# A decode step of attention and feed-forward: 72 rows of thirty value tiles weighed row by row on ScalarE and summed on GpSimd, and 56 rows left to TensorE

## The chip, the cores and the metric

The kernel runs on one core of one Trainium2 chip. A core has five engines that run their own queues of instructions in order: TensorE (PE), VectorE (DVE), ScalarE (ACT), GpSimd (POOL) and SyncE (SP), which here issues the DMAs. The metric is the device time of one execution in microseconds (us); lower is better. The kernel before takes 1319.18 us, the median of three runs (1319.18 to 1319.35).

## The reference

Four sequences (B = 4) decode one token each. A modulation vector scales and shifts a layer norm; 32 heads of 128 attend over 4096 cached positions; a feed-forward layer with SiLU follows. All is float32, and nearly all bytes are the two caches, 268 MB each.

```python
mod = (_silu(c) @ w_mod).reshape(c.shape[0], 6, 1, -1)
sa, ca, ga, sb, cb, gb = (mod[:, i] for i in range(6))
h = _layernorm(x, axis=-1) * (1 + ca) + sa
q = (h @ wq).reshape(B, Sq, H, Dh).transpose(0, 2, 1, 3)
scores = jnp.einsum("bhqd,bhkd->bhqk", q, k_cache) * (Dh ** -0.5)
p = _softmax(scores, axis=-1)
o = jnp.einsum("bhqk,bhkd->bhqd", p, v_cache)
x = x + ga * (o.transpose(0, 2, 1, 3).reshape(B, Sq, H * Dh) @ wo)
h = _layernorm(x, axis=-1) * (1 + cb) + sb
x = x + gb * (_silu(h @ w1) @ w2)
```

## The kernel before

**Tiles.** The loop `for n in range(N)` runs over 32 tiles. Tile n holds four heads (group t = n // 4) of one sequence (b = n % 4): Kn and Vn are each one load of 8.39 MB, 128 partitions by 128 rows of 128 numbers. A head has 32 partitions, and a partition has 128 neighbouring positions (NJ = 128 rows). Below, "K16" or "V14" is the tile of that n.

**Scores.** `mult` multiplies K by the query in place, rows 0 to 39 on GpSimd (NA = 40; the query is in SBUF, `qw`), the other 88 on VectorE (the query is in PSUM, `qb`); line L280 is both. `red` (L285) sums each row on VectorE: first its own 88 rows, then GpSimd's 40. `rowmax`, `bmax` (a transpose on PE, L293) and `negmax` (L298 to L301) find the largest score of each head; `softexp` takes Exp on ScalarE (L307), with the sums of a tile in column b of `rs`, and writes the weights on GpSimd (L311) into the padded masks `pz`, 16 columns for each set of four rows (JJ = 4).

**Values.** For tiles 0 to 29 (`first(n)` is not 0), `vmult` weighs the first NV = 32 rows on GpSimd with one product of 4096 numbers a partition (L323), and folds them to four rows by three sums of 2048, 1024 and 512 (L327). `vsum` adds those four rows into the accumulator `po` by a matmul with a mask of heads (L333), and `pv` multiplies the other 96 rows by `pz`, four rows a matmul, 24 matmuls (L348; each matmul appears twice in the trace). Tiles 30 and 31 leave all 128 rows to `pv`.

**Order.** The program writes the order of each engine by hand; no scheduler moves anything. One iteration n issues, in this order: the load of K(n+1); the K products of n; the query of n+1 (`make_qb`, on ScalarE L275, and at the last tile of a group L269); `vmult` and `pv` of n-1; the reductions of n; the load of Vn; `rowmax` and `bmax` of n; `vsum` of n-1; `negmax` and `softexp` of n. Three buffers of 64 KB a partition (`bufs=3`) hold all tiles: Vn takes the buffer of Kn when that is reduced, and K(n+1) takes the buffer of V(n-2) when `vsum(n-2)` is done. The loads land in the order K(n), V(n-1), K(n+1), V(n), and all are issued from SyncE's queue (L85).

**Group work.** At b = 3 the iteration also runs `gather(t, 0)` and `norm(t)`. `norm` adds the softmax sums of the group by a matmul on PE, and then VectorE takes the reciprocal. For groups 0 to 3 (t < TA = 4) that is the matmul L383, the reciprocal L386 and a product of two small SBUF tensors, L387 (32x32). For groups 4 to 7 it is the matmul L392, a product with a PSUM operand (L394), a reduction (L396) and a reciprocal (L397). On PE these matmuls stand behind `vsum(n-1)`; on VectorE they stand ahead of the next tile's K product. At b = 1 comes `gather(t-1, 1)`, at b = 2 `spread(t-1)`.

Of the kernel before, what the change touches and what calls it, by code (L numbers as in the profile page):

```python
# [10 lines left out]
AF = mybir.ActivationFunctionType  # L11
# [6 lines left out]
def kernel(  # L18
# [10 lines left out]
    nc = tc.nc  # L29
    P = 128  # L30
    B, H, S, Dh = kc.shape
# [12 lines left out]
    JJ = 4  # L44
    NG = NJ // JJ
    HG = NG // 2
# [4 lines left out]
    FG = F // G  # L51
    NA = 40
    NL = 56
    NV = 32
    SCALE = 1.0 / math.sqrt(Dh)
    EPS = 1e-5
    N = B * NT
# [29 lines left out]
    kt, vt = {}, {}  # L87
# [189 lines left out]
    sc, nm, po, rs = {}, {}, {}, {}  # L277
# [25 lines left out]
    def softexp(n):  # L303
        t, b = divmod(n, B)
        if b == 0:
            rs[t] = work.tile([P, B], F32, tag="rs", name=f"rs{t}")
        nc.scalar.activation(sc[n], sc[n], AF.Exp, bias=nm[n], accum_out=rs[t][:, b : b + 1])  # L307
        for h in range(2):
            f = first(n) if h == 0 else 0
            m = HG - f  # L310
            nc.gpsimd.tensor_mul(  # L311
                pz[h][:, f * W : HG * W].rearrange("p (g x) -> p g x", g=m)[:, :, E:].rearrange("p g (i j) -> p g i j", i=HP),
                sc[n][:, JJ * (HG * h + f) : HG * JJ * (h + 1)].rearrange("p (g j) -> p g j", j=JJ)
                .unsqueeze(2).to_broadcast([P, m, HP, JJ]),
                hm.unsqueeze(1).unsqueeze(3).to_broadcast([P, m, HP, JJ]),
            )

    def first(n):
        return NV // JJ if n < N - 2 else 0

    def vmult(n):
        if first(n):
            nc.gpsimd.tensor_mul(  # L323
                vt[n][:, :NV, :], vt[n][:, :NV, :], sc[n][:, :NV].unsqueeze(2).to_broadcast([P, NV, Dh])
            )
            for m in (NV // 2, NV // 4, JJ):
                nc.gpsimd.tensor_add(vt[n][:, :m, :], vt[n][:, :m, :], vt[n][:, m : 2 * m, :])  # L327

    def vsum(n):
        t, b = divmod(n, B)  # L330
# [103 lines left out]
    for n in range(N):  # L434
# [6 lines left out]
        w, m = (NJ // 2, NL // 2) if n == 0 else (NJ, NL) if n == 1 else (NJ, NA)  # L441
        for lo in range(0, NJ, w):
            mult(nc.gpsimd, qw, n, lo, lo + m)
            mult(nc.vector, qb, n, lo + m, lo + w)
            if n + 1 < N and not lo:
                make_qb(n + 1)
            if n:
                vmult(n - 1)
                pv(n - 1)
            red(n, lo + m, lo + w)  # L450
# [14 lines left out]
        if n and first(n - 1):  # L465
            vsum(n - 1)
        negmax(n)
        softexp(n)
        if b == 3:
            gather(t, 0)  # L470
# [94 lines left out]
```

## Time and profile before

The profiled execution took 1319.24 us; its span, from the first to the last instruction, is 1317.5 us. The page's rows of busy time:

| engine | busy us | share of the span | instructions |
|---|---|---|---|
| VectorE | 1029.0 | 78% | 361 |
| GpSimd | 848.6 | 64% | 227 |
| TensorE matmuls | 381.3 | 29% | 2114 |
| ScalarE | 51.4 | 4% | 164 |
| loads | 567.30 MB read | 431 GB/s over the span | 11408 packets |

A share is an average over the whole span; what matters in one stage is what ends last there. A row of the timeline has start, duration, engine, line, operation and tiles, and in brackets how long the engine had been idle and what ended that. A row that ends in x3 merges three instructions. The query for one line gives the shortest, median and longest duration in ns.

### The profile page before, as it was taken

To read this page: it belongs to the slowest core of one execution; us is meant where nothing else is said; L and a number is where in the kernel's file an instruction comes from. 1 tells how busy PE (TensorE), PEld (TensorE's weight loads), DVE (VectorE), ACT (ScalarE), POOL (GpSimd) and SP (SyncE) were. 2 spreads that over 40 slices of the span, in tenths; PEclk is the share of its full clock that TensorE was granted. 3 is DMA by queue.
4 is the path that set the end of the run, shared out by engine and by line. 5 is a ranking of instruction groups with operands and counts; after the bars stand their busy time and mean duration, and the time that the engine had idled before them with its cause. 6 is when DMAs were issued, how large, how long until landed. Compare 5 with 4: busy or idle time off the path is not lost.

```text
span 1317.5 us, 5429 instructions
## 1 busy us (share of the span) xinstructions
PE 381.3 (29%) x2114; PEld 104.2 (8%) x2114; DVE 1029.0 (78%) x361; ACT 51.4 (4%) x164; POOL 848.6 (64%) x227
## 2 busy tenths in 40 slices
PE   3402333221222232133222123232312332221357
PEld 0100000000000000000000001000000000000013
DVE  2597788987877888788888887789887888977852
ACT  1100000000000000000000000000000000000001
POOL 0457767666876766687676677667667767666800
PEclk9756666655666665566665566666556666555668
DMA  9999999999999999999999999999999999999998
GB/s 414 436 422 446 434 424 442 422 440 442 420 442 432 432 438 434 434 436 428 436 438 430 430 440 434 430 436 438 426 438 438 428 432 438 434 432 438 428 428 344
DMA packets 11433, 567.65 MB, mean 431 GB/s; under 512 B 1280, under 2 KB 1296, under 8 KB 2192
## 3 DMA queue, kind: packets, MB, share of 16 engines
q1 hardware_dynamic: 11408, 567.31, 99.5%
q8 instruction: 17, 0.28, 0.1%
q14 instruction: 8, 0.07, 0.0%
HBM read 567.30 MB, written 0.01 MB: 431 GB/s over the span
## 4 chain that ended last, share of the span: by engine, by line
DMA 58%; DVE 25%; POOL 12%; PE 4%; issue 1%; ACT 0%; DVEq 0%; SPq 0%; POOLq 0%; ACTq 0%
DMA k<-in_A_k_cache_dram 31%; DMA v<-in_A_v_cache_dram 25%; DVE sc L285 14%; DVE k L280 10%; POOL v L327 6%; POOL v L323 5%; DMA wq<-in_A_wq_dram 3%; PE po L333 1%; PE po L348 1%; PE q L246 1%; PE acc L423 0%; PE q L506 0%; PE acc L428 0%; PE po L516 0%; PE mx L256 0%
## 5 line engine op out<-in xcount | busy, mean ns | idle before, releaser
L285 DVE TENSOR_REDUCE sc<-k 128x88 f32<-128x11264 f32 (+3 forms) x66 | 553.1, 8422 | 3.2
L280 DVE TENSOR_TENSOR k<-k,q 128x11264 f32<-128x11264 f32 (+2 forms) x33 | 376.3, 11402 | 169.8 <-DMA k<-in_A_k_cache_dram 155.5
L280 POOL TENSOR_TENSOR k<-k,qw 128x5120 f32<-128x5120 f32 (+2 forms) x33 | 361.8, 10964 | 123.5 <-DMA k<-in_A_k_cache_dram 92.1
L348 PE MATMUL po<-v,pz 128*32 128x512 f32 x1568 | 243.6, 786 | 645.4 <-DMA v<-in_A_v_cache_dram 645.4
L323 POOL TENSOR_TENSOR v<-v,sc 128x4096 f32<-128x4096 f32 x30 | 211.1, 7036 | 241.5 <-DMA v<-in_A_v_cache_dram 241.5
L327 POOL TENSOR_TENSOR v<-v 128x2048 f32<-128x2048 f32 (+2 forms) x90 | 243.5, 2705 | 7.1
L348 PEld LDWEIGHTS po<-v,pz 128*32 128x32 f32 x1568 | 64.7, 140 | 831.7 <-issue 831.7
L333 PE MATMUL po<-v,hs 128*32 128x512 f32 x60 | 57.4, 1060 | 140.6 <-POOL v L327 140.6
L311 POOL TENSOR_TENSOR pz<-sc,hm 128x128 f32<-128x128 f32 (+1 forms) x64 | 31.5, 514 | 33.7 <-ACT sc L307 33.7
L293 PE MATMUL mx<-ident,rm 128*128 128x128 f32 x32 | 11.3, 352 | 115.0 <-DVE rm L289 115.0
L307 ACT ACTIVATE sc<-sc,nm 128x128 f32<-128x128 f32 x32 | 12.8, 402 | 712.9 <-DVE nm L301 712.9
L275 ACT ACTIVATE qw<-q 128x128 f32<-128x128 f32 x32 | 8.9, 278 | 450.5 <-DVE k L280 417.4
L359 DVE TENSOR_TENSOR o<-po,jm 128x512 f32<-128x512 f32 x16 | 10.9, 682 | 14.6 <-PE po L348 14.6
L298 DVE TENSOR_REDUCE hx<-mx 128x4 f32<-128x128 f32 x32 | 9.3, 292 | 16.4 <-PE mx L293 16.4
L333 PEld LDWEIGHTS po<-v,hs 128*32 128x32 f32 x60 | 5.5, 141 | 147.3 <-POOL v L327 147.3
L365 DVE TENSOR_REDUCE s<-o 128x128 f32<-128x512 f32 x16 | 16.5, 1033 | 0.6
L299 DVE TENSOR_TENSOR hx<-hx,hn 128x4 f32<-128x4 f32 x32 | 16.0, 501 | 1.1
L293 PEld LDWEIGHTS mx<-ident,rm 128*128 128x128 f32 x32 | 4.7, 148 | 143.3 <-issue 112.3
L271 PE MATMUL q<-qm,blk 128*128 128x512 f32 x16 | 15.5, 1068 | 1.7 <-ACT qm L269 1.7
L199 PE MATMUL q<-wm 128*32 128x512 f32 x48 | 9.5, 698 | 18.9 <-DVE wm L183 18.9
L386 DVE RECIPROCAL dx<-mx 32x4 f32<-32x4 f32 x4 | 0.7, 179 | 16.7 <-PE po L333 11.9
L394 DVE TENSOR_TENSOR dx<-mx,xm 128x4 f32<-128x4 f32 x4 | 0.6, 162 | 15.7 <-PE mx L392 15.7
(113 smaller groups left out, 168.8 us busy)
## 6 DMA issues: line engine op xcount, KB each, us to landing
k<-in_A_k_cache_dram SPq DMA_DIRECT2D x2, 4096.0 KB, 51.9
wm<-in_head_dram SPq DMA_DIRECT2D x1, 6160.0 KB, 17.7
wo<-in_A_wo_dram SPq DMA_DIRECT2D x1, 4096.0 KB, 19.0
wo<-in_A_wo_dram SPq DMA_DIRECT2D x1, 3072.0 KB, 25.8
w<-in_B_w_dram SPq DMA_DIRECT2D x1, 2688.0 KB, 33.7
w<-in_B_w_dram SPq DMA_DIRECT2D x1, 1280.0 KB, 38.0
wo<-in_A_wo_dram SPq DMA_DIRECT2D x1, 1024.0 KB, 27.9
w<-in_B_w_dram SPq DMA_DIRECT2D x4, 256.0 KB, 17.5
```

Source lines behind the costliest of these rows:

```text
L246: nc.tensor.matmul(pq[i][W * g : W * (g + 1), :], hT[:, k, :], wqt[:, k, ch * CW : (ch + 1) * CW], start=k == 0, stop=k == NK - 1,)
L271: nc.tensor.matmul(p, blk.rearrange("p i x -> p (i x)"), m, start=True, stop=True)
L280: eng.tensor_mul(kt[n][:, lo:hi, :], kt[n][:, lo:hi, :], src[n].unsqueeze(1).to_broadcast([P, hi - lo, Dh]))
L285: nc.vector.tensor_reduce(sc[n][:, lo:hi], kt[n][:, lo:hi, :], axis=AX.X, op=ALU.add)
L293: nc.tensor.transpose(p, nm[n].to_broadcast([P, P]), ident)
L299: nc.vector.tensor_mul(m, m, hn)
L311: nc.gpsimd.tensor_mul(pz[h][:, f * W : HG * W].rearrange("p (g x) -> p g x", g=m)[:, :, E:].rearrange("p g (i j) -> p g i j", i=HP), sc[n ...
L323: nc.gpsimd.tensor_mul(vt[n][:, :NV, :], vt[n][:, :NV, :], sc[n][:, :NV].unsqueeze(2).to_broadcast([P, NV, Dh]))
L327: nc.gpsimd.tensor_add(vt[n][:, :m, :], vt[n][:, :m, :], vt[n][:, m : 2 * m, :])
L333: nc.tensor.matmul(po[t, q][0:W, :], hs[:, o : o + W], vt[n][:, :JJ, :].rearrange("p j d -> p (j d)"), start=False, stop=a == 1,)
L348: nc.tensor.matmul(po[t, q][W * g : W * (g + 1), :], pz[h][:, o : o + W], vt[n][:, JJ * j : JJ * (j + 1), :].rearrange("p j d -> p (j d)") ...
L365: nc.vector.tensor_reduce(s, o.rearrange("p j d -> p d j"), axis=AX.X, op=ALU.add)
```

## The change

`NV` goes from 32 to 72 and a chunk `NC` of eight rows is new. ScalarE weighs rows 0 to 71 in place, one instruction for each row, with the row's weight as a scale for each partition; after each eight rows GpSimd adds them to the first eight, and at the end folds eight to four. `pv` keeps rows 72 to 127, 14 matmuls instead of 24. `first(n)` is then 18, which is beyond the first mask's 16 sets of four rows, so that the first mask isn't written for these tiles, and 14 sets of the second are.

```diff
-    NV = 32
+    NV = 72
+    NC = 8
...
         for h in range(2):
-            f = first(n) if h == 0 else 0
+            f = min(max(first(n) - HG * h, 0), HG)
             m = HG - f
+            if not m:
+                continue
...
     def vmult(n):
         if first(n):
-            nc.gpsimd.tensor_mul(
-                vt[n][:, :NV, :], vt[n][:, :NV, :], sc[n][:, :NV].unsqueeze(2).to_broadcast([P, NV, Dh])
-            )
-            for m in (NV // 2, NV // 4, JJ):
-                nc.gpsimd.tensor_add(vt[n][:, :m, :], vt[n][:, :m, :], vt[n][:, m : 2 * m, :])
+            v = vt[n]
+            for lo in range(0, NV, NC):
+                for j in range(lo, lo + NC):
+                    nc.scalar.activation(v[:, j, :], v[:, j, :], AF.Copy, scale=sc[n][:, j : j + 1])
+                if lo:
+                    nc.gpsimd.tensor_add(v[:, :NC, :], v[:, :NC, :], v[:, lo : lo + NC, :])
+            nc.gpsimd.tensor_add(v[:, :JJ, :], v[:, :JJ, :], v[:, JJ:NC, :])
```

From `softexp` on the new file's lines are higher: Exp is L308, the sums are L331 and L332, `vsum`'s matmul L338, `pv`'s L353, and the small product of `norm` L392.

The place shown is iteration n=15, the last of group 3. On ScalarE before, from the Exp of tile 14 to the query of the tile after next (a row has line, operation, output<-inputs and shape; sc is a tile of scores, nm its negative maximum, rs the sums, qm and qw the query, s and mz belong to `gather`):

```order
L307 ACTIVATE sc_1078,rs_1011<-sc_1078,nm_1123 128x128
L269 ACTIVATE qm_1136<-qn,sel 128x128 x4
L275 ACTIVATE qw_1143<-q 128x128
L307 ACTIVATE sc_1133,rs_1011<-sc_1133,nm_1186 128x128
L369 ACTIVATE mz<-s,am 128x128 x2
L275 ACTIVATE qw_1211<-q 128x128
```

And with the change, the same stretch (v_2037 is V14, v_2166 is V15):

```order
L308 ACTIVATE sc_1935,rs_1803<-sc_1935,nm_2047 128x128
L270 ACTIVATE qm_2059<-qn,sel 128x128 x4
L276 ACTIVATE qw_2066<-q 128x128
L329 ACTIVATE v_2037<-v_2037,sc_1935 128x128 x72
L308 ACTIVATE sc_2056,rs_1803<-sc_2056,nm_2176 128x128
L374 ACTIVATE mz<-s,am 128x128 x2
L276 ACTIVATE qw_2200<-q 128x128
L329 ACTIVATE v_2166<-v_2166,sc_2056 128x128 x72
```

The 72 rows of V14 now stand ahead of the Exp of tile 15, and behind the query for tile 16.

On GpSimd before, from V14's product to the K product of tile 16 (k_1131) and V15's product:

```order
L323 TENSOR_TENSOR v_1113<-v_1113,sc_1078 128x4096
L327 TENSOR_TENSOR v_1113<-v_1113 128x2048
L327 TENSOR_TENSOR v_1113<-v_1113 128x1024
L327 TENSOR_TENSOR v_1113<-v_1113 128x512
L311 TENSOR_TENSOR pz_113<-sc_1133,hm 128x8x16
L311 TENSOR_TENSOR pz_114<-sc_1133,hm 128x16x16
L280 TENSOR_TENSOR k_1131<-k_1131,qw_1143 128x5120
L323 TENSOR_TENSOR v_1176<-v_1176,sc_1133 128x4096
```

And with the change (k_2054 is K16):

```order
L331 TENSOR_TENSOR v_2037<-v_2037 128x1024 x8
L332 TENSOR_TENSOR v_2037<-v_2037 128x512
L314 TENSOR_TENSOR pz_114<-sc_2056,hm 128x14x16
L281 TENSOR_TENSOR k_2054<-k_2054,qw_2066 128x5120
L331 TENSOR_TENSOR v_2166<-v_2166 128x1024 x8
```

Nine sums stand where the product and three sums stood, one mask product where two stood; the K product keeps its place behind them.

On PE with the change, from the matmuls of V14 to those of V15:

```order
L353 MATMUL po<-v_2037,pz_114 32x512 x14
L294 MATMUL mx<-ident,rm_2168 128x128
L338 MATMUL po<-v_2037,hs 32x512
L375 MATMUL od<-mz,s_124 32x256
L388 MATMUL mx<-rs_1803,b_120 32x4
L353 MATMUL po<-v_2166,pz_114 32x512 x14
```

Apart from 14 matmuls in place of 24 (8 with the first mask and 16 with the second), PE's order is that of before: the norm's matmul L388 stands behind `vsum`'s L338. VectorE's order does not change at all: L391 and L392 of the norm, then the K product of tile 16.

## Prediction

> **What bounds the kernel now.** I read the profiled page first for its DMA rows and its chain, then the DMA queue's own waits, then one stretch of the timeline. The page:
>
> ```profile
> q1 hardware_dynamic: 11408, 567.31, 99.5%
> ...
> DMA 58%; DVE 25%; POOL 12%; PE 4%; issue 1%; ACT 0%; DVEq 0%; SPq 0%; POOLq 0%; ACTq 0%
> ...
> v<-in_A_v_cache_dram SPq DMA_DIRECT2D x32, 28.6
> k<-in_A_k_cache_dram SPq DMA_DIRECT2D x31, 40.5
> ...
> out_dram<-w SPq DMA_DIRECT2D x1, 8.0 KB, 1.8
> ```
>
> The load queue's packets fill 99.5% of 16 engines over the span of 1317.5 us: the bytes set the time, and the other shares of the chain are work that hides under a load. What can lengthen the run is a load that is issued too late. The queue's own waits (engine, what it waited for, total, times, longest) name the two releases that decide this:
>
> ```profile
> SPq L85 <- DVE rm L289: 938.0, 32, 29.7
> SPq L85 <- PE po L333: 209.7, 30, 7.8
> ```
>
> A V load waits until VectorE has reduced the K tile whose buffer it takes; the K load after it waits for the small matmul L333, which ends the work on an older V tile. How much time each has is seen in the timeline (start, duration, engine, line) of iteration n=15, where V14 has just landed:
>
> ```profile
> 638.13 7.04 POOL L323 TENSOR_TENSOR v<-v,sc 128x4096 f32<-128x4096 f32 x1 [8.28 <-DMA v<-in_A_v_cache_dram]
> 638.19 6.89 PE L348 MATMUL po<-v,pz 128*32 128x512 f32 x48 [19.30 <-DMA v<-in_A_v_cache_dram]
> 645.24 8.27 POOL L327 TENSOR_TENSOR v<-v 128x2048 f32<-128x2048 f32 x3
> ...
> 650.05 0.40 ACT L307 ACTIVATE sc<-sc,nm 128x128 f32<-128x128 f32 x1 [30.79 <-DVE nm L301]
> ...
> 653.47 0.97 POOL L311 TENSOR_TENSOR pz<-sc,hm 128x128 f32<-128x128 f32 x2
> 653.56 1.06 PE L333 MATMUL po<-v,hs 128*32 128x512 f32 x1 [4.56 <-POOL v L327]
> ...
> 655.51 0.33 SPq L85 DMA_DIRECT2D k<-in_A_k_cache_dram  x1
> 655.60 0.19 DVE L386 RECIPROCAL dx<-mx 32x4 f32<-32x4 f32 x1 [3.97 <-PE po L333]
> 655.82 0.19 DVE L387 TENSOR_TENSOR ra<-dx,dqm 32x32 f32<-32x32 f32 x1
> 657.49 11.03 POOL L280 TENSOR_TENSOR k<-k,qw 128x5120 f32<-128x5120 f32 x1 [3.05 <-DMA k<-in_A_k_cache_dram]
> 657.50 11.89 DVE L280 TENSOR_TENSOR k<-k,q 128x11264 f32<-128x11264 f32 x1 [1.49 <-DMA k<-in_A_k_cache_dram]
> ...
> 669.49 17.28 DVE L285 TENSOR_REDUCE sc<-k 128x88 f32<-128x11264 f32 x2
> 676.79 7.03 POOL L323 TENSOR_TENSOR v<-v,sc 128x4096 f32<-128x4096 f32 x1 [8.27 <-DMA v<-in_A_v_cache_dram]
> ...
> 686.80 0.33 SPq L85 DMA_DIRECT2D v<-in_A_v_cache_dram  x1
> ```
>
> One period is 676.79 - 638.13 = 38.66 us for a K and a V of equal size, so 19.33 us a load. V16, issued at 686.80, lands 28.6 us later, at 715.4; its own bytes begin to count at 715.4 - 19.33 = 696.1, when K17 ends. From issue to landing a small DMA needs 1.8 us (the output row). So V16 may be issued up to 696.1 - 1.8 = 694.3: **VectorE has 7.5 us of slack**. K17, issued at 655.51, is needed when V15 lands at 676.79, so until 675.0: 19.5 us of slack. To be seen as well: in this iteration, the fourth of a group of four, VectorE waits 3.97 us for PE at L386 and 1.49 us for K16.
>
> **The change part by part.** *Thirty tiles on ScalarE.* The nearest rows are copies of one 128x128 tile with a per-partition scale from SBUF, L269, and copies from PSUM with a constant scale, L213 (first the single durations, minimum, median and maximum; then two runs of four):
>
> ```profile
> L269 ACT ACTIVATE qm<-qn,sel x32: 384/386/402, 47.2 to 1079.5; 128x128 f32<-128x128 f32 x32
> 613.22 1.28 ACT L269 ACTIVATE qm<-qn,sel 128x128 f32<-128x128 f32 x4 [1.25 <-DVE oa L407]
> 36.56 0.79 ACT L213 ACTIVATE mod<-q 128x128 f32<-128x128 f32 x4 [7.10 <-PE q L211]
> ```
>
> Four in 1.28 us with 0.386 each start (1.28 - 0.386)/3 = 0.298 us apart. L269 has the same operands, so I take 0.298: 72 rows need 71 x 0.298 + 0.386 = 21.5 us. The ends are 0.17 apart (L213: four in 0.79) and 0.386 (no overlap, 27.8 us).
>
> *GpSimd.* The product of 7.04 us and three sums go; eight sums of 1024 elements and one of 512 come, both forms in the trace:
>
> ```profile
> L327 POOL TENSOR_TENSOR v<-v 128x2048 f32<-128x2048 f32 x30 | 135.3, 4510 | 2.4
> L327 POOL TENSOR_TENSOR v<-v 128x1024 f32<-128x1024 f32 x30 | 70.3, 2344 | 2.4
> L327 POOL TENSOR_TENSOR v<-v 128x512 f32<-128x512 f32 x30 | 37.9, 1263 | 2.4
> L311 POOL TENSOR_TENSOR pz<-sc,hm 128x256 f32<-128x256 f32 x34 | 20.8, 614 | 20.4 <-ACT sc L307 20.4
> ```
>
> The three sums take 8.27 in a row against 8.12 of their own, so a gap is 0.08. The first new sum needs 16 rows: 15 x 0.298 + 0.386 = 4.9 us after landing. Eight follow at 2.42 us, as fast as ScalarE makes eight rows (8 x 0.298 = 2.38), then 1.26: **the tile is done 4.9 + 19.4 + 1.3 = 25.6 us after landing, at 663.7 instead of 653.5**, 10.2 us later. The two mask products (0.97 us) become one of 224 elements, at most 0.61.
>
> *What this moves in every iteration.* K17 is issued at 665.7, inside its 19.5 us; without that cover each us too late would cost 30 us in all. The Exp L307 stands behind the rows on ScalarE, at 659.7 instead of 650.05; the mask product reads it, but that now waits for the sums anyway. GpSimd's K product starts at 663.7 + 0.7 = 664.4 instead of 657.49, for K16 is there, and ends at 675.4; VectorE needs it only after reducing its own part, at 669.49 + 11.89 = 681.4. Ten of 24 matmul groups go, from a PE that waits 19.30 us for V: nothing. So 23 of the 30 iterations cost nothing.
>
> *The fourth iteration of each group.* Here VectorE needs the softmax sums: L386 reads a matmul that stands on PE behind L333, so behind the new last sum. Behind L386 on VectorE wait L387 and then the whole K product, whose reduction releases V16. L386 comes at 655.60 + 10.2 = 665.8 and L387 at 666.0. But GpSimd has by then been in its 11.03 us K product since 664.4, which before started after L387. What VectorE does then is read from another small product of two SBUF tensors, L299, in iteration n=1 (its statistics over the run; then GpSimd's three sums and L299 there), with L387's own statistics:
>
> ```profile
> L299 DVE TENSOR_TENSOR hx<-hx,hn x32: 161/508/1475, 78.7 to 1268.8; 128x4 f32<-128x4 f32 x32
> ...
> 104.48 8.27 POOL L327 TENSOR_TENSOR v<-v 128x2048 f32<-128x2048 f32 x3
> 107.53 1.48 DVE L299 TENSOR_TENSOR hx<-hx,hn 128x4 f32<-128x4 f32 x1
> ...
> L387 DVE TENSOR_TENSOR ra<-dx,dqm x4: 178/182/188, 193.0 to 655.8; 32x32 f32<-32x32 f32 x4
> ```
>
> It takes 0.161 us alone and up to 1.475. GpSimd's first sum ended at 104.48 + 4.51 = 108.99, and L299 at 109.01: it stood until GpSimd's instruction was over. L387 never met one. I take it that L387, with two SBUF inputs as well, now stands until 675.4. VectorE's K product then starts at 675.5 instead of 657.50, 18.0 us late, and V16 is issued at 704.8. It lands at 704.8 + 1.8 + 19.33 = 725.9 instead of 715.4: **10.5 us without a load**. There are four such iterations (n = 3, 7, 11, 15): 42 us.
>
> The rule behind that row: the Trainium skill, "SBUF — State Buffer", section "Who interferes with whom", says that a VectorE instruction with two SBUF inputs and a GpSimd instruction that reads SBUF exclude each other, and that whichever is second waits for the whole of the first. L299's end, 0.02 us after GpSimd's, agrees.
>
> In the second half of the groups the norm is another one (n = 19, 23, 27; here n=27, V26 landing at 1103.25):
>
> ```profile
> 1110.36 8.28 POOL L327 TENSOR_TENSOR v<-v 128x2048 f32<-128x2048 f32 x3
> ...
> 1121.98 0.16 DVE L397 RECIPROCAL rd<-rd 128x1 f32<-128x1 f32 x1
> 1122.57 11.89 DVE L280 TENSOR_TENSOR k<-k,q 128x11264 f32<-128x11264 f32 x1 [0.43 <-DMA k<-in_A_k_cache_dram]
> ```
>
> Its product L394 reads PSUM and one SBUF tensor, as does the large K product L280, which runs beside GpSimd's at its usual 11.89. So I let it pass. L397 ends 3.5 us after GpSimd's sums (1118.64), now at 1103.25 + 25.6 + 3.5 = 1132.35; K starts at 1132.4, 9.8 late, against a slack of 7.5: 2.3 us each, 7 us in three.
>
> *Does one delay bring the next?* After n=15, ScalarE's qw copy stands behind VectorE's K product, to 687.8, so V15's sums end at 713.4 and GpSimd's K17 product at 725. VectorE starts K17 at about 708 and releases V17 at about 737.5; it is needed by 725.9 + 19.3 - 1.8 = 743.4. It does not. Tiles 30 and 31 keep the old path, so the tail stays.
>
> Sum: 42 + 7 = 49 us on the profiled execution, which took 1319.24 us (span and 1.7 around it; the median of the runs is 1319.18): **1368 us**.
>
> **The rivals.** *A: no exclusion at L387.* Against: L299. VectorE then starts K at 666.3, 8.8 late against 7.5: 1.3 us four times and 2.3 three times, 12 us, 1331 us. *B: the other norm stands still too,* if L394, L396 or L397 excludes GpSimd's product. For: no row shows them beside a GpSimd instruction. K starts 18.4 late, 10.9 us three times: 42 + 33, 1394 us. By the rule of the Trainium skill named above, an instruction with one SBUF input does not contend, which speaks against B. *C: ScalarE's rows don't overlap.* Sums end 6 us later, in all seven iterations: 49 + 42, 1410 us. Against: the run of four. *D: not slower; the slack covers it.* Place: L387 and the 7.5 us. If it isn't excluded and rows start 0.17 apart, the first sum starts at 2.9 and the tile is done at 23.6 us, 8.2 later; K starts 6.8 late in the first half, inside the slack, and 0.3 us late three times in the second: 1320 us. It decides where the sums end less than 8.9 us later than now. For: constant-scale copies run so. Against: these have a scale from SBUF.
>
> **How the numbers follow.** Forecast 0.68; A 0.11; B 0.08; C 0.05; D 0.05; and 0.03 for a gain that no row here shows. About 0.2% is what a measurement of this kernel can tell from no change, 2.6 us. Slower: 0.68 + 0.11 + 0.08 + 0.05 = 0.92; same 0.05; faster 0.03. The range takes in the forecast, A and B with two or three us beyond: 1328 to 1396. Within it lies the forecast with rows at 0.17, 2 us less at seven places, 1354.
>
> **What would show it.** In the changed profile ScalarE's rows should be 0.386 each and 21.5 a tile; GpSimd's last sum 25.6 us after landing; the 32x32 product of the norm (four times) about 9 us long, ending with GpSimd's K product; four V loads landing some 21 us after issue and three about as much, the others 28.6; the share of the load queue near 96%. I am wrong if that product stays near 0.2 us, if a VectorE wait shows in other iterations, or if V loads are late with VectorE on time.

## The result and the profile after

The changed kernel takes **1378.24 us** (median of four runs, 1377.3 to 1379.46) against 1319.26 us before (four runs): 1.0444 times as long [1.0431, 1.0457]. The profiled execution took 1379.46 us, its span is 1377.7 us.

The page of the changed kernel, with the data rates of 40 slices, the DMA queues (packets, MB, share of 16 engines) and the chain by engine:

```profile
GB/s 417 434 426 426 445 433 282 426 426 453 427 295 440 427 426 443 288 426 427 438 440 280 427 446 434 426 398 428 425 428 396 426 427 447 432 379 445 427 425 340
...
q1 hardware_dynamic: 11408, 567.31, 95.7%
q8 instruction: 12, 0.20, 0.1%
q14 instruction: 28, 0.23, 0.0%
...
DMA 40%; DVE 27%; POOL 20%; ACT 5%; PE 4%; issue 4%; SPq 0%; DVEq 0%; ACTq 0%; POOLq 0%
```

The same packets and bytes as before fill 95.7% of the span instead of 99.5%. Four slices fall to 280 to 295 GB/s, and three to 379 to 398: seven places where the load engines ran dry. The chain has 40% of DMA where it had 58%, and GpSimd rose from 12% to 20%. The two rows of kind `instruction` will matter below, where q14's packets go with the number of ScalarE's instructions and q8's with PE's; I take them for the loading of the engines' code. Before, they read:

```profile
q8 instruction: 17, 0.28, 0.1%
q14 instruction: 8, 0.07, 0.0%
```

What SyncE's queue waited for, after (total, times, longest):

```profile
SPq L86 <- DVE rm L290: 783.5, 32, 38.7
SPq L86 <- PE po L338: 471.2, 30, 18.1
```

The K loads now wait up to 18.1 us for PE's small matmul (7.8 before). That is 10.3 us more, inside their slack of 19.5 us. What costs time is the longest wait of a V load, 38.7 us in place of 29.7. The iteration of the prediction, n=15, in the timeline after, with V14 landing at 673.73 by its first `pv` matmul:

```profile
673.66 21.14 ACT L329 ACTIVATE v<-v,sc 128x128 f32<-128x128 f32 x72 [9.53 <-DMA v<-in_A_v_cache_dram]
673.73 5.71 PE L353 MATMUL po<-v,pz 128*32 128x512 f32 x28 [9.97 <-DMA v<-in_A_v_cache_dram]
...
678.53 19.34 POOL L331 TENSOR_TENSOR v<-v 128x1024 f32<-128x1024 f32 x8 [7.25 <-ACT v L329]
...
697.94 1.26 POOL L332 TENSOR_TENSOR v<-v 128x512 f32<-128x512 f32 x1
...
699.68 10.96 POOL L281 TENSOR_TENSOR k<-k,qw 128x5120 f32<-128x5120 f32 x1
...
701.29 0.19 DVE L391 RECIPROCAL dx<-mx 32x4 f32<-32x4 f32 x1 [13.66 <-PE po L338]
701.51 9.17 DVE L392 TENSOR_TENSOR ra<-dx,dqm 32x32 f32<-32x32 f32 x1
710.72 11.89 DVE L281 TENSOR_TENSOR k<-k,q 128x11264 f32<-128x11264 f32 x1
...
712.31 5.19 PE L353 MATMUL po<-v,pz 128*32 128x512 f32 x28 [11.14 <-DMA v<-in_A_v_cache_dram]
...
740.02 0.33 SPq L86 DMA_DIRECT2D v<-in_A_v_cache_dram  x1
...
762.05 5.92 PE L353 MATMUL po<-v,pz 128*32 128x512 f32 x28 [11.66 <-DMA v<-in_A_v_cache_dram]
```

Read from the bottom: V16 lands 762.05 - 712.31 = 49.74 us after V15, where two loads need 38.63. It was issued at 740.02, and its landing 22.0 us later says that nothing was ahead of it (28.6 us where a load stands ahead). It was issued late because VectorE began its K product at 710.72 instead of as K16 landed; and VectorE was held by L392, a product of 32x32 numbers that took 9.17 us and ended at 710.68, 0.04 us after GpSimd's K product (699.68 + 10.96 = 710.64).

**Where the 60.2 us are.** The difference of the spans (1377.7 - 1317.5) can be booked by the intervals between the landings of neighbouring V tiles, 38.63 us in an undisturbed period. V0 to V30 make 30 of them. I take the seven in which the second V load waits for the K product that stands behind a `norm` on VectorE (n is the iteration of that norm), and the 23 others. What they have over 38.63 us each:

| kernel | median us | n=3, 7, 11, 15 | n=19, 23, 27 | these seven | the 23 others | q14 packets |
|---|---|---|---|---|---|---|
| before | 1319.26 | 0 each | 0 to 0.1 | 0.0 | 1.6 | 8 |
| after | 1378.24 | 10.7, 9.9, 11.5, 11.1 | 3.2, 2.9, 3.2 | 52.5 | 8.4 | 28 |
| norm through PSUM | 1344.63 | 2.5, 2.0, 2.5, 2.5 | 2.9, 3.1, 3.1 | 18.6 | 8.8 | 28 |
| 56 rows | 1350.57 | 5.9, 7.6, 7.1, 5.3 | 0, 0, 0.3 | 26.1 | 7.3 | 24 |
| norm early | 1328.3 | 0, 0, 0.7, 0 | 0.7, 0.6, 0.9 | 2.8 | 8.1 | 28 |
| norm early, 40 rows | 1322.43 | 0, 0, 0.8, 0 | 0.8, 0, 0.7 | 2.1 | 3.0 | 18 |
| before, norm early | 1319.28 | 0.5, 0, 0, 0 | 0 each | 0.3 | 2.5 | 9 |
| the same + 72 rows | 1328.65 | 0, 0, 0.7, 0 | 0.7, 0, 0.7 | 1.9 | 8.2 | 25 |
| the same + 18 wide instructions | 1319.37 | 0.2, 0, 0, 0 | 0 each | 0.0 | 2.5 | 12 |
| before, VectorE held | 1392.04 | 9.7, 8.0, 9.0, 9.1 | 8.7, 9.6, 9.9 | 64.0 | 10.2 | 8 |
| the same + 72 rows | 1465.89 | 24.5, 23.9, 24.8, 24.6 | 13.3, 13.7, 13.6 | 138.3 | 9.9 | 25 |

For the changed kernel: 43.3 us at the first four, 9.3 at the other three, 8.4 - 1.6 = 6.8 in ordinary iterations, and 1.0 in the tail (from V30's landing to the end), less 0.1 ahead of V0: 60.3 together. The other rows are the experiments, but for one that failed.

### The profile page after: what moved, and what is told of

Same layout as the page of the kernel before. It is cut to its first block, busy times and chain, and to the rows that moved or that the text cites. A ratio compares the mean times of both kernels' runs of the same rounds, so it can differ in the third digit from the quotient of the medians.

```text
span 1377.7 us, 6781 instructions
## 1 busy us (share of the span) xinstructions
PE 325.1 (24%) x1514; PEld 87.2 (6%) x1514; DVE 1080.2 (78%) x361; ACT 680.0 (49%) x2324; POOL 981.6 (71%) x347
## 3 DMA queue, kind: packets, MB, share of 16 engines
q1 hardware_dynamic: 11408, 567.31, 95.7%
## 4 chain that ended last, share of the span: by engine, by line
DMA 40%; DVE 27%; POOL 20%; ACT 5%; PE 4%; issue 4%; SPq 0%; DVEq 0%; ACTq 0%; POOLq 0%
POOL v L331 19%; DMA k<-in_A_k_cache_dram 19%; DMA v<-in_A_v_cache_dram 16%; DVE k L281 14%; DVE sc L286 12%; ACT v L329 5%; DMA wq<-in_A_wq_dram 3%; PE po L338 2%; DMA wo<-in_A_wo_dram 2%; POOL v L332 1%; PE q L247 1%; PE acc L433 0%; PE q L511 0%; PE po L521 0%; PE od L380 0%
## 5 line engine op out<-in xcount | busy, mean ns | idle before, releaser
L331 POOL TENSOR_TENSOR v<-v 128x1024 f32<-128x1024 f32 x240 | 564.1, 2351 | 270.1 <-ACT v L329 253.7
L329 ACT ACTIVATE v<-v,sc 128x128 f32<-128x128 f32 x2160 | 634.2, 388 | 182.9 <-DMA v<-in_A_v_cache_dram 182.9
L353 PE MATMUL po<-v,pz 128*32 128x512 f32 x968 | 185.6, 876 | 350.5 <-DMA v<-in_A_v_cache_dram 350.5
L338 PE MATMUL po<-v,hs 128*32 128x512 f32 x60 | 57.4, 1060 | 397.7 <-POOL v L332 397.7
L353 PEld LDWEIGHTS po<-v,pz 128*32 128x32 f32 x968 | 47.0, 152 | 495.7 <-issue 495.7
L294 PE MATMUL mx<-ident,rm 128*128 128x128 f32 x32 | 13.6, 425 | 266.9 <-DVE rm L290 266.9
L391 DVE RECIPROCAL dx<-mx 32x4 f32<-32x4 f32 x4 | 0.7, 179 | 55.5 <-PE po L338 41.0
L332 POOL TENSOR_TENSOR v<-v 128x512 f32<-128x512 f32 x30 | 38.0, 1267 | 2.4
L314 POOL TENSOR_TENSOR pz<-sc,hm 128x224 f32<-128x224 f32 (+1 forms) x34 | 19.1, 565 | 27.4 <-ACT sc L308 27.4
L308 ACT ACTIVATE sc<-sc,nm 128x128 f32<-128x128 f32 x32 | 12.5, 390 | 52.2 <-DVE nm L302 52.2
L392 DVE TENSOR_TENSOR ra<-dx,dqm 32x32 f32<-32x32 f32 x4 | 35.9, 8982 | 0.1
L300 DVE TENSOR_TENSOR hx<-hx,hn 128x4 f32<-128x4 f32 x32 | 32.5, 1014 | 1.1
L338 PEld LDWEIGHTS po<-v,hs 128*32 128x32 f32 x60 | 5.4, 140 | 406.0 <-POOL v L332 406.0
```

Of the source, the lines that this page charges most:

```text
L294: nc.tensor.transpose(p, nm[n].to_broadcast([P, P]), ident)
L300: nc.vector.tensor_mul(m, m, hn)
L314: nc.gpsimd.tensor_mul(pz[h][:, f * W : HG * W].rearrange("p (g x) -> p g x", g=m)[:, :, E:].rearrange("p g (i j) -> p g i j", i=HP), sc[n ...
L329: nc.scalar.activation(v[:, j, :], v[:, j, :], AF.Copy, scale=sc[n][:, j : j + 1])
L331: nc.gpsimd.tensor_add(v[:, :NC, :], v[:, :NC, :], v[:, lo : lo + NC, :])
L332: nc.gpsimd.tensor_add(v[:, :JJ, :], v[:, :JJ, :], v[:, JJ:NC, :])
```

## The experiments

**The norm's product with one SBUF input.** Theory: the exclusion at L392 makes the four long gaps. The reciprocal is written to PSUM, and L392 reads one operand there; nothing else is changed.

```diff
         if t < TA:
+            m = psum([P, B], "mx", 2)
...
-            m = work.tile([P, B], F32, tag="dx", name="dx")
```

> The changed kernel, with one edit: the reciprocal of the norm of groups 0 to 3 (L391) is written to PSUM, so that the small product behind it (L392) has one SBUF input instead of two. Theory X (a product of two SBUF tensors on VectorE stands until GpSimd's running instruction is over): L392 takes 0.2 us instead of 9.0, VectorE's K product starts 9 us earlier in four iterations, and some 2 us are left of each of their gaps, so 1378 - 4 x 8.8 = 1343 us (1338 to 1348). Rival Y (L392 is long because it waits for something else that is late in that iteration, PE or the K tile): L392 or the instruction behind it keeps its 9 us, and the time stays at 1378.

Measured: 1344.63 us (1344.32 to 1345.09), 1.019 times before [1.0175, 1.0205]. The timeline of this kernel in the same iteration n=15:

```profile
674.43 11.02 POOL L281 TENSOR_TENSOR k<-k,qw 128x5120 f32<-128x5120 f32 x1
...
676.05 0.21 DVE L391 RECIPROCAL mx<-mx 32x4 f32<-32x4 f32 x1 [13.64 <-PE po L338]
676.29 0.20 DVE L392 TENSOR_TENSOR ra<-mx,dqm 32x32 f32<-32x32 f32 x1
676.51 11.89 DVE L281 TENSOR_TENSOR k<-k,q 128x11264 f32<-128x11264 f32 x1
```

GpSimd is in its K product all the same, and L392 takes 0.20 us in the middle of it. The four gaps shrink from 10.8 us on average to 2.4, and 33.6 us go with one operand moved. What is left of them goes with the lateness of the sums; the run after next, in which VectorE no longer waits for the sums, leaves no gap.

**Fewer rows.** If the four gaps follow the end of GpSimd's K product, two sums fewer (4.8 us) shorten each by about as much; if the loss went with the number of rows, it would fall by a ninth for every eight.

```diff
-    NV = 72
+    NV = 56
```

> The changed kernel with 56 rows on ScalarE and GpSimd in place of 72 (NV = 56), the rest with TensorE. Two sums of 2.42 us fewer: the last sum 20.8 us after landing in place of 25.6, GpSimd's K product 4.8 us earlier at both ends. By the exclusion of the norm's product L392 (theory X) VectorE's K product waits for GpSimd's: 13.2 us late in place of 18.0, so four gaps of about 6 us instead of 10.8; in the other three iterations K starts 5 us late, inside the slack of 7.5, and no gap is left. Sum 1319.5 + 4 x 6 + about 5 us of code loading and realigned loads = 1348 us, 1340 to 1352, with some 22 to 24 packets on q14. By a theory in which the whole loss goes with the number of rows, 59 us x 56/72 = 46 us: 1365 us.

Measured: 1350.57 us (1349.89 to 1351.14), 1.0232 times [1.0215, 1.0249], against 1348 forecast and 1365 by the rival. The statistics of L392 (minimum, median, maximum in ns):

```profile
L392 DVE TENSOR_TENSOR ra<-dx,dqm x4: 8655/9423/9428, 197.4 to 682.5; 32x32 f32<-32x32 f32 x4
```

The product still stands out GpSimd's; only its place in time is earlier. The four gaps are 6.5 us on average, 4.3 less than with 72 rows, and the three of the second half are gone: with sums 4.8 us earlier they lie inside the slack, but for 0.3 us in one. The loss is a matter of a deadline, not of the amount of work.

**The norm one iteration later, behind `bmax(n)`.** Then VectorE does it in a stretch in which it waits for K anyway, and no gap should be left. The question was whether the changed kernel then costs nothing (theory G) or whether something remains that goes with the rows (rival S).

```diff
+        if t and b == 0:
+            norm(t - 1)
...
-            norm(t)
+            if n == N - 1:
+                norm(t)
```

> The changed kernel with the norm of a group moved by one iteration: it is issued ahead of vsum's matmul in the first iteration of the next group (the last group keeps its place), so that VectorE no longer waits for the new last sum. All 2160 rows on ScalarE and all sums on GpSimd stay. If all that the change costs comes from VectorE's late start in the fourth iterations (theory X, and theory G: the 8 us that the other iterations lost come with the gaps in the load stream), no load is late and the time is 1319 to 1322 us, with V landings 38.6 us apart. Rival S (ScalarE's rows slow the loads by themselves, by their traffic or the loading of their code): the gaps go but the 8 us stay, 1327 to 1329 us, with single intervals near 39.7 us.

Measured: 1328.3 us (1327.94 to 1329.42), 1.0069 times [1.0052, 1.0086]. No gap is left, and the load queue is busy for 99.2% of the span. Theory G fell: 9 us stay, spread over iterations in which every V load was issued in time (none lands less than 28.5 us after its issue from V2 on). Sixteen of the 30 intervals are 39.2 to 39.5 us, nearly all others 38.6. My prediction had no term for this. The page of this kernel:

```profile
q1 hardware_dynamic: 11408, 567.31, 99.2%
q8 instruction: 12, 0.20, 0.1%
q14 instruction: 28, 0.23, 0.0%
```

Two causes offer themselves: 20 more packets of instructions (q14) for an engine with 2160 more of them, and the traffic of ScalarE in SBUF. (On q8 there are 5 fewer, 12 for 17: its packets follow the number of PE's matmuls, 2114 before and 1514 here.) The next runs part them.

**ScalarE's rows added to the kernel before.** First try, with all 72 results of a tile written to one scratch row that nobody reads:

```diff
+            for j in range(72):
+                nc.scalar.activation(scr, vt[n][:, NV + j, :], AF.Copy, scale=sc[n][:, j : j + 1])
```

> The kernel before, with 72 extra ScalarE rows for each of tiles 0 to 29: each reads a row of V (rows 32 to 103, which stay as they are), scales it by a score and writes it to one scratch tile that nobody reads. The Exp and the norm stand behind the rows, 21.5 us after landing, so VectorE's K product is some 5 us late in the fourth iterations, inside its slack of 7.5. Theory G: the loads don't notice the rows, 1319 to 1321 us. Rival S: the rows slow the loads, 1327 us or more, in intervals without a gap.

Measured: 1417.77 us (1415.85 to 1417.96), 1.0741 times [1.0725, 1.0757], a miss of both. The timeline of ScalarE in this kernel, two rows:

```profile
654.66 31.26 ACT L325 ACTIVATE scr<-v,sc 128x128 f32<-128x128 f32 x72 [6.26 <-DMA v<-in_A_v_cache_dram]
685.82 0.39 ACT L308 ACTIVATE sc<-sc,nm 128x128 f32<-128x128 f32 x1
```

Rows that all write one place don't overlap: 31.26 / 72 = 0.434 us each, where the changed kernel has (21.14 - 0.387) / 71 = 0.292 from start to start. The Exp behind them came 10 us later still, GpSimd's K product with it, and the norm was excluded: gaps of 16.6 to 18.5 us four times and 6.2 to 6.8 three times. The run says nothing on the question.

So the norm was put early in the kernel before as well, and that kernel is the base for the next two:

> The kernel before, with the norm moved by one iteration as in the run of the changed kernel with an early norm. It is the control for that one and the base of the next two. Nothing was late before, so all theories expect the time of before: 1318 to 1321 us, V landings 38.6 us apart, and 8 blocks of ScalarE's code on the instruction queue of the page (q14).

Measured: 1319.28 us (1319.08 to 1320.54), 0.9999 times [0.999, 1.0008]: the move alone does nothing, as expected. On it, 72 rows for each of thirty tiles, into 16 scratch places in turn:

```diff
+            for j in range(72):
+                nc.scalar.activation(scr[:, j % 16, :], vt[n][:, NV + j, :], AF.Copy, scale=sc[n][:, j : j + 1])
```

> That control with 72 extra rows on ScalarE for each of tiles 0 to 29, this time into 16 scratch places in turn (in the run before, one place made each row wait for the last). The products and sums on GpSimd stay as they were; rows 32 to 103 of V are only read, and nobody reads the results. No V load should be late. Theory C (the 9 us that the changed kernel with an early norm still lost are the loading of ScalarE's code: 28 packets on q14 instead of 8, which take turns with the loads on the same DMA engines): about 28 packets on q14 and 1326 to 1330 us, in single intervals of 39.2 to 39.3 us. Theory P (they come from GpSimd's or VectorE's new schedule, for example a later K load): 1318 to 1321 us.

Measured: 1328.65 us (1327.62 to 1329.51), 1.0066 times [1.0049, 1.0082]. The 9 us are there, with GpSimd's and PE's instructions as in the base. GpSimd's K product starts 3.2 us later, for the Exp stands behind the rows, but every V load is issued in time (28.5 us or more ahead of its landing). And the same bytes by a quarter of the instructions, on the same base:

```diff
+            for j in range(18):
+                nc.scalar.activation(
+                    scr[:, j % 4, :], vt[n][:, NV + 4 * j : NV + 4 * j + 4, :].rearrange("p j d -> p (j d)"), AF.Copy
+                )
```

> The control with the same bytes read by ScalarE in 18 instructions of four rows each for a tile, with a constant scale, into scratch. 540 instructions in all instead of 2160. Theory C: about 12 packets on q14 and 1319 to 1322 us. Theory T (ScalarE's traffic to and from SBUF slows the loads): as much as with 72 rows, 1326 us or more.

Measured: 1319.37 us (1319.17 to 1320.34), 1.0 times [0.999, 1.0009]. The pages of these two, first the 72 rows:

```profile
q14 instruction: 25, 0.20, 0.0%
```

and the wide ones, with the row of the timeline that shows them:

```profile
q14 instruction: 12, 0.10, 0.0%
```

```profile
676.79 9.47 ACT L325 ACTIVATE scr<-v 128x512 f32<-128x512 f32 x18 [7.04 <-DMA v<-in_A_v_cache_dram]
```

Traffic falls as a cause: the same bytes, moved in 9.5 us instead of 21.1, cost nothing. What costs goes with the number of instructions. (These copies also lack the scale from SBUF; no run parts that from their number.) A last point on that line is the changed kernel with early norm and 40 rows:

```diff
-    NV = 72
+    NV = 40
```

> The changed kernel with an early norm and 40 rows on ScalarE instead of 72 (NV = 40), so 1200 rows in all, and 88 rows left to TensorE. Theory C: the loss goes with the packets of ScalarE's code, about 17 on q14, so 9 us x (17 - 8) / (28 - 8) = 4 us: 1322 to 1325 us. Theory P or T: no simple relation to the packets; P gives 1319 if the sums end as early as in the kernel before (they end about 16 us after landing).

Measured: 1322.43 us (1321.95 to 1323.41), 1.0022 times [1.0013, 1.0031]. Without gaps, the packets of q14 and the times are 9: 1319.28, 12: 1319.37, 18: 1322.43, 25: 1328.65 and 28: 1328.3. So 16 packets more cost 9.4 us (0.6 us each), 9 more cost 3.2 (0.35 each), 3 more nothing. That the loading of ScalarE's code slows the load stream is what fits all five.

The traces also hold the start of each instruction packet, and they bear this out. Take the 23 others of the table's eleven kernels, 253 intervals. Of the 75 in which no packet starts, on q8 or q14, 2 are 0.3 us or more over 38.63; of the 178 in which one does, 83 are. In the run with 72 rows alone, each of the 15 long intervals, of all 30, holds a q14 packet, and six with such a packet aren't long. How a packet does it shows in the sixteen parts in which a load lands: in that run they end 2.6 to 2.8 us apart up to V6, and with each of the first seven long intervals 0.6 to 0.7 us further apart, up to 7.0 at V17. So some parts are held up and others not, and the load counts as landed with its last part. Why 0.65 us, when such a packet takes 0.31 itself, stays open.

**A gap without the change.** Are the 8.4 us of the changed kernel the same 9 us? The kernel before was given a reduction of 17.2 us behind `norm` on VectorE in seven iterations, so that V loads come late with no instruction added on ScalarE:

```diff
+            if n < N - 1:
+                nc.vector.tensor_reduce(
+                    scr, qn.unsqueeze(1).to_broadcast([P, P, Dh]), axis=AX.X, op=ALU.add
+                )
```

> The kernel before, with one extra reduction on VectorE behind the norm in seven iterations (n = 3 to 27): 16384 elements a partition, written to a scratch tile that nobody reads, 17.1 us by the duration of the K reduction (11.89 us for 11264). It makes gaps in the load stream without a row on ScalarE. VectorE's K product starts 15.7 us late four times and 16.7 us three times; less 7.5 us of slack, plus 0.9 us that each gap was longer than forecast in the changed kernel, the gaps are 9.1 and 10.1 us, 67 us in all. Theory G (each gap also costs about 1.2 us in the iterations that follow): 1319 + 67 + 8 = 1394 us, and single intervals of V landings near 39.7. Rival S: no loss beside the gaps, 1386 us, all other intervals 38.6.

Measured: 1392.04 us (1391.64 to 1392.34), 1.0549 times [1.0533, 1.0565]. The seven gaps sum to 64.0 us, against 67 forecast; and beside them, with 8 packets on q14 as before, the ordinary intervals have 10.2 us too much, 39.0 to 40.1 us for several of those that follow a gap. So a gap has an aftermath without ScalarE's rows, 10.2 - 1.6 = 8.6 us for seven. The packets' starts tell more of it: after each of the seven gaps, the longest ordinary interval is the first in which a q8 packet starts, one of PE's code. These seven hold 8.3 of the 10.2 us. Before, the same packets cost nothing but once (1.55 us between V18 and V19). What a gap leaves behind is thus, by these records, a stream that PE's next packet slows; no run takes PE's packets away, so that much is argued. Both at once:

```diff
+            for j in range(72):
+                nc.scalar.activation(scr2[:, j % 8, :], vt[n][:, NV + j, :], AF.Copy, scale=sc[n][:, j : j + 1])
```

> The kernel before with both additions at once: the 17.1 us reduction behind norm in seven iterations, as in the run with held VectorE alone (1392.0 us), and 72 rows of ScalarE for each of thirty tiles into eight scratch places in turn, as in the run with rows alone (1328.7 us, 9 us more than without). The rows' results are used by nobody. What is asked is whether the two leftovers add up where a kernel has both, as the changed kernel does. If they add: seven gaps of 64 us in all, some 10 us of realigned loads and some 9 us of code loading, 1399 to 1403 us, about 25 packets on q14. If the slack that a gap leaves in the load engines takes up the code loads, as the changed kernel's 8.4 us for both suggests: 1390 to 1396 us with the same number of packets. The condition for either is that GpSimd's K product stays out of the way: the Exp of a tile comes some 12 us later behind the rows, GpSimd's K product too, and VectorE must still have its small product of norm done before that starts.

Measured: 1465.89 us (1465.39 to 1466.5), 1.1107 times [1.109, 1.1123]. As a time it is a miss: the condition named in the expectation broke. The timeline of iteration n=3 of this kernel shows how:

```profile
195.11 0.68 ACT L373 ACTIVATE mz<-s,am 128x128 f32<-128x128 f32 x2
...
195.84 1.06 PE L374 MATMUL od<-mz,s 128*32 128x256 f32 x2 [4.81 <-ACT mz L373]
196.20 10.97 POOL L282 TENSOR_TENSOR k<-k,qw 128x5120 f32<-128x5120 f32 x1
...
196.99 0.17 DVE L390 RECIPROCAL dx<-mx 32x4 f32<-32x4 f32 x1 [9.82 <-PE mx L387]
197.20 10.02 DVE L391 TENSOR_TENSOR ra<-dx,dqm 32x32 f32<-32x32 f32 x1
207.15 17.20 DVE L477 TENSOR_REDUCE scr<-qn 128x128 f32<-128x16384 f32 x1
```

ScalarE's copy L373 for `gather` stands behind the rows and the Exp; PE's matmul L374 waits for it, the norm's matmul behind that one, and VectorE reaches its small product after GpSimd has begun. The same exclusion, by another road, makes the gaps 13 to 25 us. The question asked is answered all the same: the 23 ordinary intervals have 9.9 us, no more than the 10.2 without the rows. With gaps, which are longer here, ScalarE's code loads add nothing that can be seen.

## Why the prediction was right, point by point

**The bound and the slack held.** Loads issued in time cost nothing through their issue. K17 at n=15 was issued at 701.24 - 673.73 = 27.5 us after V14's landing, as worked out (665.7 - 638.1 = 27.6).

**ScalarE and GpSimd held.** The rows of the changed kernel, from the query for one line:

```profile
L329 ACT ACTIVATE v<-v,sc x2160: 384/387/403, 97.2 to 1298.0; 128x128 f32<-128x128 f32 x197
```

That is 0.387 each, 0.292 apart and 21.14 us a tile (0.298 and 21.5 forecast). GpSimd's last sum ends at 699.20, 25.5 us after landing (25.6). This is what rival C (no overlap) and rival D (sums less than 8.9 us later) needed otherwise.

**The fourth iteration, first half, held.** The expected product of about 9 us is there four times:

```profile
L392 DVE TENSOR_TENSOR ra<-dx,dqm x4: 8406/9174/9176, 203.0 to 701.5; 32x32 f32<-32x32 f32 x4
```

It ends with GpSimd's K product, 36.9 us after V14's landing (675.4 - 638.1 = 37.3 forecast). The four gaps sum to 43.3 us against 42, and the run with the norm through PSUM, where they sum to 9.5, shows that 33.8 us hang on that product's second SBUF input: that run is rival A made real. The rule of the Trainium skill ("SBUF — State Buffer", "Who interferes with whom") agrees with both: the form with two SBUF inputs waited until GpSimd's instruction of 10.96 us was over, 9.17 us, and the form with one passed beside it in 0.20 us.

**The second half held.** There the norm has no product with two SBUF inputs. Its rows in n=27, in the timeline after:

```profile
1184.10 11.01 POOL L281 TENSOR_TENSOR k<-k,qw 128x5120 f32<-128x5120 f32 x1
...
1186.58 0.16 DVE L399 TENSOR_TENSOR dx<-mx,xm 128x4 f32<-128x4 f32 x1 [14.53 <-PE mx L397]
1186.78 0.16 DVE L401 TENSOR_REDUCE rd<-dx 128x1 f32<-128x4 f32 x1
1186.97 0.16 DVE L402 RECIPROCAL rd<-rd 128x1 f32<-128x1 f32 x1
1187.08 11.89 DVE L281 TENSOR_TENSOR k<-k,q 128x11264 f32<-128x11264 f32 x1
```

They pass beside GpSimd in 0.16 us each, so rival B falls. K starts 28.9 us after V26's landing at 1158.15 (1132.4 - 1103.25 = 29.2 forecast). The three gaps are 9.3 us against 7.

**Two terms were mis-sized**, 11.4 us of the 60.3. First the slack. I took 1.8 us from issue to the first byte that counts, from the row of a small DMA. A late V load lands 21.9 to 22.5 us after its issue, so this part is 2.6 to 3.2 us beyond the 19.33 of its bytes. Each gap is 0.8 to 1.4 us longer for it, 1.0 on average, so that VectorE's slack is nearer 28.6 - 22.1 = 6.5 us than 7.5; VectorE was 0.2 to 0.4 us earlier than worked out (n=27 and n=15), and 3.6 us remain in seven gaps. Second, **"so 23 of the 30 iterations cost nothing"** failed in size: no load is late in them, as I argued, and yet they have 6.8 us more than before, and the tail 1.0. (The tail may not be the change's: the profiled execution of the kernel before with an early norm has it too, 60.6 us from V30's landing to the end as here, against 59.6 before.) I had costed the additions on ScalarE by who waits for ScalarE, and never by what the load engines carry for it. Either of two causes makes such a leftover by itself: the code of 2160 more instructions (9 us where there are no gaps) and the aftermath of gaps (8.6 us for seven longer ones). In one kernel they don't add (9.9 us for both). In the changed kernel, the seven intervals that hold the first q8 packet after a gap have 6.8 of the 8.4 us, as with VectorE held (8.3 of 10.2). That points to the aftermath; but four of the seven hold q14 packets too, and how the 6.8 us divide stays open.

No version beat the kernel before. Its loads fill 99.5% of the span, and the changed kernel with the norm early is 9 us slower with 72 rows, 3 us with 40.

## What to carry to other kernels

Where loads fill the span, ask of each engine's added work which release it delays, and set that against the slack of the load behind it: here 10.2 us on GpSimd were free in 23 iterations and decided the other seven. Where VectorE and GpSimd overlap, look at small VectorE products with two SBUF inputs that stand ahead of a long GpSimd instruction: 0.18 us became 9.17 because the order of the two had turned over. And count instructions as well as their time: 2160 small ones on an engine that was 4% busy slowed a saturated load stream by 9 us, and a quarter as many with the same bytes by nothing.

## What the runs showed of the hardware

- **Loading instructions can slow a saturated load stream.** With the loads at 99.2 to 99.5% of the span, 16 more packets of about 8 KB on q14 went with 9.4 us, in single intervals some 0.65 us longer. The Trainium skill, "Runtime: NRT & Kernel Launch", section "Instruction fetch mechanics", has each engine fetch its instructions by a DMA queue of its own and calls the cost of a block's end mostly hidden. For the engine itself the trace agrees (rows 0.292 us apart, 72 in a row); for the loads beside it the runs don't (1328.65 against 1319.28 us).
- **A gap has an aftermath.** After a load stream ran dry, some of the next intervals were up to 1.4 us longer (40.07 against 38.63 with VectorE held), with nothing late, and the longest after each gap was the first with a packet of PE's code. In the trace, the sixteen parts of a load end 2.3 to 3.8 us apart before and 0.5 to 0.8 us apart right after a gap with VectorE held; where that packet starts, the next load's parts end 0.8 to 1.4 us further apart than that. That the packet holds up some of the parts is argued from this, not shown.
- **ScalarE's rows of 0.387 us overlapped when they wrote to different places**: 0.292 us apart in place or over 16 scratch rows, 0.434 into one.
- **From issue to landing on an idle queue** a load of 8.39 MB took 21.9 to 22.5 us, 2.6 to 3.2 more than its 19.33 us in a full queue.
